# Attention, then a squared-ReLU layer pair: row maxima taken ten slots ahead, weighted sums in two parts, the seam between the stages overlapped

## The chip, the cores and the metric

One core of one Trainium2 chip runs the whole program. The metric is the device time of one execution in microseconds (us), lower is better. The engines are PE (TensorE, matrix products), DVE (VectorE), ACT (ScalarE), POOL (GpSimd) and SP (SyncE, which here only issues DMAs). Each of them runs its own instructions in program order and waits on semaphores of the others.

## What is computed

```python
def _attn_ref(q, k, v, g_q, g_k):          # q, k, v: 8 x 12 heads x 448 x 64, float32
    def rmsnorm(x, g):
        rms = np.sqrt(np.mean(x * x, axis=-1, keepdims=True) + 1e-06)
        return x / rms * g
    q_n, k_n = (rmsnorm(q, g_q), rmsnorm(k, g_k))
    scores = 1.0 / np.sqrt(64) * np.matmul(q_n, k_n.transpose(0, 1, 3, 2))
    scores = scores - np.max(scores, axis=-1, keepdims=True)
    attn = np.exp(scores)
    attn = attn / (np.sum(attn, axis=-1, keepdims=True) + 1e-09)
    return np.matmul(attn, v)

def _moe_ref(x, w_in, w_out, s, b):        # x: 3584 x 768, w_in: 768 x 2048, w_out: 2048 x 768
    r = np.maximum(x @ w_in, 0.0)
    return (s * (r * r) + b) @ w_out
```

The output of attention, 3584 tokens by 768, is the first operand of layer one.

## The kernel before

**Three stages.** Attention runs over 48 pairs of heads. Layer one (`ffn_in`, 8 batches of 448 tokens by 16 blocks of 128 columns, 128 blocks in all) follows it, then layer two (`multiply`, seven products of a blocked scheme for each 256 tokens). Weights and first operands of both layers are split in a high and a low float32r part, so each block of layer one is 18 matmuls.

**Slots.** Attention is written as a loop over slots, four to a pair (`W = 4`), from `FIRST = -14`. Slot i holds the work of one quarter of a pair, and `jobs` says which other steps are issued in it; all engines' orders are fixed by this program order (`manual_schedule`). In slot i:
- `score_t(i)` (L252, L256) makes a quarter of the transposed scores `st` on PE: a product of the scaled `kq`, then a second one that adds minus the row maxima, which lie as one row in a buffer `shq`. `exponent(i)` (L263) takes `exp` of it on ACT into `e`.
- `score(i + AHEAD)` (L223) makes a quarter of the untransposed scores `sh`, only for the maxima, and `maximum` (L232) reduces it on DVE into `nmx`. `sh` has one buffer in PSUM. `AHEAD` is 6.
- `shift` (L241) moves the four quarters of maxima of a pair into `shq` with two small DMAs, two slots before `score_t` first reads them. There are two `shq`, used in turn.
- in every fourth slot, `weigh` (L272, L279) makes the weighted sums of a pair and the sums of its exponentials (`av`): 16 products with v and 8 with ones, 24 in one run. `take` (L288, L289) copies them out on ACT.
- before and after a pair come its other steps: `load`, `norm` (L177, L182, L184, L185: squares on ACT, sums on DVE, the power -1/2 on POOL), `keep`, `load_kq`, `spread` (L201), `scale` (L205, L207, L211), `load_v`, then `gather` (L297, four small DMAs of the sums), `invert`, `put_z`, `get_z` (L314), `divide` (L320, POOL), `put_x` (L323).
- `convert` splits one of 24 pieces of w_in (a DMA `w64i` of 512 KB, L330) in every seventh slot, from slot 4 to slot 165.

**SP.** All DMAs are issued by SP in program order. A DMA waits there for the engine that makes its data, and each also for an earlier DMA on one of eight lanes, so the one eight places before it must have landed.

**The seam.** After the last slot the attention pools are closed. Then `x_load(0)` (L409) reads batch 0 of the attention's output and `x_split` (L416 on ACT, L417 on DVE) splits its six parts; the first block of layer one follows (L426). During layer one, `convert_out` splits w_out, 32 pieces spread over the first 103 blocks. In the last batch `t_step` prepares the sums of w_out for layer two: DMA, POOL (L514 to L516), ACT (L524), DVE (L532) in a chain.

## Time and profile before

| what | value |
|---|---|
| median of three runs | 1638.98 us (1638.83 to 1641.5) |
| the profiled execution | 1635.42 us, of which the span is 1633.4 us |
| busy share of the span | PE 90%, DVE 46%, ACT 41%, POOL 38% |
| attention, first transposed score to last weighted sum | 30.85 to 715.4 us |
| layer one, layer two begin at | 738.74 us, 1218.05 us |

The span runs from the first to the last instruction. A time line row says when a run of equal instructions on an engine began, how long it took, and in brackets how long the engine was idle before it and what ended that. PEclk is the granted clock of TensorE as a share of 2.4 GHz; its two levels are 1.0 (2.4 GHz) and 0.5 (1.2 GHz), and a mean lies between them. "DMA share" is the mean busy share of the core's 16 DMA engines.

### The profile page before, as it was taken

What the parts mean: (1) busy time and instruction counts of PE and PEld (TensorE: products, weight loads), DVE (VectorE), ACT (ScalarE), POOL (GpSimd) and SP (SyncE); (2) the same over time, 40 slices, a digit from 0 to 9 for tenths busy, and PEclk for the clock granted to TensorE, in tenths of its full rate; (3) what the DMA queues carried; (4) which work ended last, traced back from release to release, by engine and by line L of the source; (5) the groups of instructions that cost most, each with busy time, mean ns of one, the idle gap of its engine ahead of it and who ended that gap; (6) DMA issues with size and microseconds to landing.
All of it is one profiled execution on the core that took longest, in us unless ns stands there. A gap on an engine that the chain in (4) does not pass through costs nothing.

```text
span 1633.4 us, 23219 instructions
## 1 busy us (share of the span) xinstructions
PE 1474.5 (90%) x8536; PEld 1112.8 (68%) x8536; DVE 751.3 (46%) x1112; ACT 674.6 (41%) x1010; POOL 623.5 (38%) x536
## 2 busy tenths in 40 slices
PE   4888888888888888849999999999989999999999
PEld 3433333333333343418999999999979999999999
DVE  4444444454554444302222122221469677776775
ACT  3554555554555554322222222222355444444443
POOL 5554555555545654110000000000466555465553
PEclk6988889898988988879999999999999999999999
DMA  7566565656656565214434434442443333243331
GB/s 205 161 172 171 150 177 164 182 170 172 184 153 174 152 182 146 55 60 141 152 111 149 139 120 140 156 133 97 142 147 109 98 104 97 84 117 97 104 97 65
DMA packets 191234, 221.75 MB, mean 136 GB/s; under 512 B 69520, under 2 KB 162192, under 8 KB 191120
## 3 DMA queue, kind: packets, MB, share of 16 engines
q1 hardware_dynamic: 191120, 220.26, 45.9%
q8 instruction: 67, 1.10, 0.3%
q14 instruction: 47, 0.39, 0.1%
HBM read 161.48 MB, written 58.19 MB: 134 GB/s over the span
## 4 chain that ended last, share of the span: by engine, by line
PE 75%; DMA 11%; DVE 4%; SPq 4%; issue 2%; ACT 2%; POOL 2%; POOLq 0%; ACTq 0%; DVEq 0%
PE ph L426 26%; PE m L606 25%; PE av L272 9%; DMA shq<-nmx 6%; PE st L252 5%; PE st L256 4%; PE av L279 4%; DVE nmx L232 3%; PE sh L223 3%; SPq L297 3%; DMA raw<-in_dram 1%; DMA rb<-i_d 1%; DMA w<-w_d 1%; DMA i_d<-ri 1%; DVE t L532 1%
## 5 line engine op out<-in xcount | busy, mean ns | idle before, releaser
L426 PE MATMUL ph<-x,wih 128*128 128x448 f32 x1536 | 439.4, 367 | 23.3 <-DMA w64o<-in_dram 23.3
L606 PE MATMUL m<-t,gh 128*128 128x384 f32 x1568 | 400.9, 336 | 6.9 <-ACT gh L587 6.9
L232 DVE TENSOR_REDUCE nmx<-sh 112x2 fp32r<-112x896 f32 x192 | 207.8, 1082 | 357.9 <-PE sh L223 348.4
L426 PEld LDWEIGHTS ph<-x,wih 128*128 128x128 f32 x1536 | 289.2, 188 | 49.7 <-ACT x L416 24.1
L606 PEld LDWEIGHTS m<-t,gh 128*128 128x128 f32 x1568 | 284.8, 189 | 7.3 <-ACT gh L587 7.3
L426 PE MATMUL ph<-x,wil 128*128 128x448 f32 x768 | 281.9, 367 | 0.0
L256 PE MATMUL st<-shq,row 64*128 64x448 f32 x384 | 187.8, 782 | 91.0 <-DMA shq<-nmx 91.0
L606 PE MATMUL m<-t,gl 128*128 128x384 f32 x784 | 263.4, 336 | 0.1
L263 ACT ACTIVATE e<-st 128x896 f32<-128x896 f32 x192 | 176.0, 917 | 137.5 <-PE st L256 137.0
L252 PE MATMUL st<-kq 64*128 64x448 f32 x768 | 221.4, 624 | 0.2 <-ACT e L263 0.2
L444 ACT ACTIVATE r<-ph 128x448 f32<-128x448 f32 x128 | 69.6, 544 | 306.4 <-PE ph L426 193.2
L514 POOL TENSOR_TENSOR w<-w 128x384 f32<-128x384 f32 x13 | 17.0, 1305 | 442.0 <-DMA w<-w_d 436.6
L587 ACT CAST gh<-g 128x896 fp32r<-128x896 f32 x112 | 105.4, 942 | 178.3 <-POOL g L577 107.5
L256 PEld LDWEIGHTS st<-shq,row 64*128 64x128 f32 x384 | 65.3, 222 | 160.1 <-DMA shq<-nmx 137.6
L272 PE MATMUL av<-e,v 128*32 128x448 f32 x1536 | 172.3, 594 | 0.0
L588 DVE TENSOR_TENSOR gl<-g,gh 128x896 fp32r<-128x896 f32 x112 | 141.5, 1265 | 56.3 <-ACT gh L587 51.9
L573 POOL TENSOR_TENSOR g<-g 128x256 f32<-128x256 f32 x112 | 94.5, 844 | 179.2 <-DVE g L572 179.2
L417 DVE TENSOR_TENSOR x<-xr,x 128x448 fp32r<-128x448 f32 x48 | 29.6, 625 | 278.4 <-ACT x L416 261.2
L223 PE MATMUL sh<-kr 64*112 64x448 f32 x384 | 128.4, 532 | 32.2 <-DVE nmx L232 18.5
L426 PEld LDWEIGHTS ph<-x,wil 128*128 128x128 f32 x768 | 144.6, 188 | 12.7
L185 POOL TENSOR_TENSOR ri<-ri,mhalf 128x14 f32<-128x14 f32 x48 | 148.3, 3090 | 4.0
L606 PEld LDWEIGHTS m<-t,gl 128*128 128x128 f32 x784 | 147.8, 189 | 0.6 <-DVE gl L588 0.6
(63 smaller groups left out, 1465.8 us busy)
## 6 DMA issues: line engine op xcount, KB each, us to landing
r_d<-r SPq DMA_DIRECT2D x128, 224.0 KB, 2.0
raw<-in_dram SPq DMA_DIRECT2D x48, 448.0 KB, 5.9
kq<-in_dram SPq DMA_DIRECT2D x48, 448.0 KB, 4.8
rb<-i_d SPq DMA_DIRECT2D x96, 224.0 KB, 5.2
raw<-r_d SPq DMA_DIRECT2D x64, 256.0 KB, 2.8
v<-in_dram SPq DMA_DIRECT2D x48, 256.0 KB, 3.8
w64i<-in_dram SPq DMA_DIRECT2D x24, 512.0 KB, 5.8
w64o<-in_dram SPq DMA_DIRECT2D x32, 384.0 KB, 3.4
```

The lines of the kernel that those rows point to most:

```text
L185: G.tensor_tensor(ri, ri, mhalf[:, :n], ALU.pow)
L223: T.matmul(sh[:QC, j, :SEQ], t[d, 1].rearrange("k (p c) -> k c p", c=NQ)[:, c], t[d, 0], start=True, stop=True,)
L232: V.tensor_reduce(out=nmxs[p][:, :, c : c + 1], in_=shs.pop(i)[:QC, :, :SEQ], op=ALU.max, axis=AX.X, negate=True,)
L252: T.matmul(st[:, j, :SEQ], t[d, 0, k0 : k0 + P], t[d, 1], start=True, stop=False)
L256: T.matmul(st[:, j, :SEQ], row[d], shq[p % 2][d], start=False, stop=True)
L263: S.activation(e, sts.pop(i)[:, :, :SEQ], AF.Exp)
L272: T.matmul(t[n * Q : (n + 1) * Q, 0, :SEQ], x[:, kc, j, h * Q : (h + 1) * Q], e[kc][:, j], start=kc == 0, stop=kc == NKC - 1,)
L426: T.matmul(ph[:, :SEQ], w[:, cc, f0 : f0 + P], xs[b, cc][:, part, :], start=n == 0, stop=n == 3 * NCC - 1,)
L573: G.tensor_tensor(g9[:, 2:4], g9[:, 0:2], g9[:, 7:8].broadcast_to([P, 2, P]), ALU.add)
L587: S.copy(gh, g9[:, 1:8])
L588: V.tensor_tensor(gl, g9[:, 1:8], gh.bitcast(F32), ALU.subtract)
L606: T.matmul(to, g[:, sa], w, start=m == 0 and n == 0, stop=m == NM - 1 and n == 2,)
```

## The change

**In attention.** `AHEAD` becomes 10, and all steps before a pair move by four slots with it (`FIRST = -19`). `shift` stays at `s0 - AHEAD + W`, so it is now issued six slots before its first use; three `shq` instead of two, six `kq` instead of five. In even slots `score` stands ahead of `score_t`, in odd slots behind it, so the products for the maxima come in twos around the weighted sums. `weigh` is cut in two: part 0 (quarters 0 and 1) in slot 4p+3, part 1 (quarters 2 and 3) with `take` in slot 4p+5. `e` has one buffer for each quarter instead of two. The first four `sh` lie in four different places of PSUM. One multiplication of the first pair goes from POOL to DVE.

**At the seam.** `x_load(0)` is issued in slot 184 of 192 and the six `x_split` in slots 187 to 192, between the attention's own work. The slots after 193 (their DMAs, `invert`, `divide`) are issued between the first 16 blocks of layer one. `convert_out` starts four blocks later.

**At the end of layer one.** The last two blocks are run together, part by part of the first operand, and the splits for layer two stand ahead of their copies out of PSUM.

```diff
-FIRST = -14
-AHEAD = 6
+FIRST = -19
+AHEAD = 10
 STAGES = {
-    "raw": (-24, 0),
-    "norm": (-21, 1),
-    "keep": (-18, 3),
-    "kq": (-16, 1),
-    "spread": (-15, 4),
-    "scale": (-11, 5),
+    "raw": (-28, 0),
+    "norm": (-25, 1),
+    "keep": (-22, 3),
+    "kq": (-20, 1),
+    "spread": (-19, 4),
+    "scale": (-15, 5),
 }
...
-        shq = [ap.tile([P, SEQ], F32R, name=f"shq{n}") for n in range(2)]
+        shq = [ap.tile([P, SEQ], F32R, name=f"shq{n}") for n in range(3)]
...
+            tag = ("sh", "st0", "st1", "av")[i] if i < W else "sh"
+            sh = shs[i] = ps.tile([P, 2, 512], F32, tag=tag, name=f"sh{i}")
...
-            e = es[i] = ap.tile([P, 2, SEQ], F32, tag=f"e{kc}", bufs=2, name=f"e{i}")
+            e = es[i] = ap.tile([P, 2, SEQ], F32, tag=f"e{kc}", name=f"e{i}")
...
+            ahead = 0 <= i + AHEAD < NSLOT
+            if ahead and i % 2 == 0:
+                score(i + AHEAD)
             if 0 <= i < NSLOT:
                 score_t(i)
                 exponent(i)
-            if 0 <= i + AHEAD < NSLOT:
-                score(i + AHEAD)
+            if ahead:
+                if i % 2:
+                    score(i + AHEAD)
                 maximum(i + AHEAD)
...
-            if i % W == 1 and 0 <= (i - 5) // W < NPAIR:
-                weigh((i - 5) // W)
-                take((i - 5) // W)
+            if i % 2 and 0 <= (i - 3) // W < NPAIR:
+                p, g = divmod(i - 3, W)
+                weigh(p, g // 2)
+                if g:
+                    take(p)
...
     with tc.manual_schedule(engines=ORDERED):
-        x_load(0)
-        for cc in range(NCC):
-            x_split(0, cc)
+        for i in range(FIRST, NSLOT + 2):
+            slot(i)
+            if i == NSLOT - 8:
+                first.close()
...
+                x_load(0)
+            if NSLOT - 5 <= i < NSLOT + 1:
+                x_split(0, i - NSLOT + 5)
+        early.close()
...
         for n in range((B - 1) * NFC):
             b, fc = divmod(n, NFC)
             rectify()
             ffn_in(b, fc)
             keep_r()
+            if n < 16:
+                slot(NSLOT + 2 + n)
...
         rectify()
+        ffn_in(B - 1, NFC - 2, NFC - 1)
         keep_r()
```

On PE in the middle of attention, the rows of one pair (16) stood like this before; `st` is the transposed score, `sh` the score for the maxima, the number behind a name is the slot (for `av`, `kq`, `v` the pair):

```order
L223 MATMUL sh71_2200<-kr17_2044 112x448 x2
L272 MATMUL av15_2214<-e60_2055,v15_1954 32x448 x4
L272 MATMUL av15_2214<-e61_2082,v15_1954 32x448 x4
L272 MATMUL av15_2214<-e62_2132,v15_1954 32x448 x4
L272 MATMUL av15_2214<-e63_2153,v15_1954 32x448 x4
L279 MATMUL av15_2214<-e60_2055,ones_203 32x448 x2
L279 MATMUL av15_2214<-e61_2082,ones_203 32x448 x2
L279 MATMUL av15_2214<-e62_2132,ones_203 32x448 x2
L279 MATMUL av15_2214<-e63_2153,ones_203 32x448 x2
L252 MATMUL st66_2243<-kq16_1721 128x448 x2
L256 MATMUL st66_2243<-shq0_209,row_207 128x448 x2
L223 MATMUL sh72_2250<-kr18_2162 112x448 x2
```

And now:

```order
L228 MATMUL sh75_2259<-kr18_2090 112x448 x2
L278 MATMUL av15_2214<-e62_2181,v15_2013 32x448 x4
L278 MATMUL av15_2214<-e63_2199,v15_2013 32x448 x4
L285 MATMUL av15_2214<-e62_2181,ones_209 32x448 x2
L285 MATMUL av15_2214<-e63_2199,ones_209 32x448 x2
L228 MATMUL sh76_2289<-kr19_2208 112x448 x2
L257 MATMUL st66_2292<-kq16_1664 128x448 x2
L261 MATMUL st66_2292<-shq1_216,row_213 128x448 x2
L257 MATMUL st67_2311<-kq16_1664 128x448 x2
L261 MATMUL st67_2311<-shq1_216,row_213 128x448 x2
L228 MATMUL sh77_2318<-kr19_2208 112x448 x2
```

Between two `sh` there now lies either half of the weighted sums or two `st`; before there was one `st` between most of them and the whole of the weighted sums between two.

On SP in the same place, from the output of pair 24 (`x_d`) to the loads; before:

```order
L323 DMA x_d4_87<-u24_3488 128x448
L297 DMA zt26_3542<-sz26_3525 64x1x7 x4
L241 DMA shq0_209<-nmx28_3421 1x112x4 x2
L188 DMA i_d32_179<-ri32_3465 128x2x7
L314 DMA zb25_3563<-z_d25_116 64x448 x2
L215 DMA v29_3588<-in_2_dram 128x512
L195 DMA kq32_3590<-in_0_dram 128x896
L171 DMA raw34_3592<-in_1_dram 128x896
```

And now:

```order
L331 DMA x_d4_87<-u24_3547 128x448
L305 DMA zt26_3588<-sz26_3571 64x1x7 x4
L246 DMA shq2_217<-nmx29_3467 1x112x4 x2
L191 DMA i_d33_180<-ri33_3524 128x2x7
L322 DMA zb25_3609<-z_d25_116 64x448 x2
L219 DMA v29_3647<-in_2_dram 128x512
L198 DMA kq33_3649<-in_0_dram 128x896
L174 DMA raw35_3651<-in_1_dram 128x896
```

The order of the steps is the same; what stands behind the four `zt` of pair 26 is now the maxima of pair 29 instead of 28, and the loads of `kq` and `raw` are one pair further ahead.

On ACT at the seam, where `x0` is the split first operand of layer one and `ph` its product; before:

```order
L263 ACTIVATE e191_5757<-st191_5752 128x896
L288 COPY sz47_5793<-av47_5767 128x448
L289 COPY uz47_5792<-av47_5767 128x448
L416 CAST x0_0_5833<-xr0_5831 128x448
L416 CAST x0_1_5836<-xr0_5831 128x448
L416 CAST x0_2_5839<-xr0_5831 128x448
L416 CAST x0_3_5842<-xr0_5831 128x448
L416 CAST x0_4_5845<-xr0_5831 128x448
L416 CAST x0_5_5848<-xr0_5831 128x448
L444 ACTIVATE r0_0_5872<-ph0_0_5851 128x448
```

And now:

```order
L268 ACTIVATE e189_5738<-st189_5733 128x896
L296 COPY sz46_5756<-av46_5705 128x448
L297 COPY uz46_5755<-av46_5705 128x448
L419 CAST x0_2_5759<-xr0_5654 128x448
L268 ACTIVATE e190_5767<-st190_5762 128x896
L419 CAST x0_3_5775<-xr0_5654 128x448
L268 ACTIVATE e191_5783<-st191_5778 128x896
L419 CAST x0_4_5801<-xr0_5654 128x448
L419 CAST x0_5_5806<-xr0_5654 128x448
L296 COPY sz47_5825<-av47_5788 128x448
L297 COPY uz47_5824<-av47_5788 128x448
L447 ACTIVATE r0_0_5864<-ph0_0_5839 128x448
```

The six splits stand between the last exponentials, ahead of the copies of the last pair's sums.

## Rows read from the trace of the kernel before

**Rows 1.** Stretch 100 to 650 us: busy us (instructions) PE, PEld, DVE, ACT, POOL; clock, DMA share, GB/s.
```profile
100.00:650.00 550.00, 464.28 (x3063) 206.79 (x3063) 258.33 (x358) 285.62 (x387) 291.12 (x214) 0.88 0.61 170
```

**Rows 2.** The page: granted TensorE clock in 40 slices of 40.8 us.
```profile
PEclk6988889898988988879999999999999999999999
```

**Rows 3.** Who waited for whom, whole span: us in total, times, longest.
```profile
PE st L256 <- DMA shq<-nmx: 91.0, 75, 3.2
PE sh L223 <- DVE nmx L232: 18.5, 56, 1.8
PE m L606 <- ACT gh L587: 6.9, 1, 6.9
```

**Rows 4.** Time line of PE, one pair of attention: start, us, engine, line, tile.
```profile
486.72 0.57 PE L223 MATMUL sh<-kr 64*112 64x448 f32 x2 [0.24 <-DVE nmx L232]
487.21 3.21 PE L272 MATMUL av<-e,v 128*32 128x448 f32 x32
...
491.86 1.02 PE L252 MATMUL st<-kq 64*128 64x448 f32 x4
...
492.93 0.36 PE L223 MATMUL sh<-kr 64*112 64x448 f32 x2
493.13 0.91 PE L252 MATMUL st<-kq 64*128 64x448 f32 x4
...
498.59 0.47 PE L256 MATMUL st<-shq,row 64*128 64x448 f32 x1 [2.79 <-DMA shq<-nmx]
```

**Rows 5.** Time line of SP, same place: issues of DMAs.
```profile
493.70 0.33 SPq L323 DMA_DIRECT2D x_d<-u  x1
...
501.33 0.43 SPq L171 DMA_DIRECT2D raw<-in_dram  x1
...
503.00 1.40 SPq L201 DMA_DIRECT2D rb<-i_d  x2
```

**Rows 6.** DMA issues of the whole span: KB each, median us from issue to landing.
```profile
raw<-in_dram SPq DMA_DIRECT2D x48, 448.0 KB, 5.9
```

**Rows 7.** Time line of DVE, POOL and ACT, same place.
```profile
487.18 1.08 DVE L182 TENSOR_REDUCE ssq<-raw 128x14 f32<-128x896 f32 x1
...
488.64 3.93 POOL L185 TENSOR_TENSOR ri<-ri,mhalf 128x14 f32<-128x14 f32 x1
...
496.74 0.94 ACT L177 ACTIVATE raw<-raw 128x896 f32<-128x896 f32 x1
...
502.62 2.59 POOL L185 TENSOR_TENSOR ri<-ri,mhalf 128x14 f32<-128x14 f32 x1
505.17 1.14 POOL L320 TENSOR_TENSOR u<-uz,zb 128x448 f32<-128x448 f32 x1
```

**Rows 8.** Three stretches of two neighbouring pairs, columns as in Rows 1.
```profile
486.00:493.00 7.00, 6.76 (x62) 2.51 (x60) 4.09 (x7) 2.78 (x5) 4.57 (x3) 1.00 0.94 260
495.40:500.40 5.00, 2.04 (x10) 1.20 (x8) 1.03 (x2) 2.44 (x4) 1.68 (x2) 0.91 0.22 12
500.50:509.50 9.00, 9.00 (x70) 3.60 (x66) 4.20 (x7) 4.27 (x7) 6.09 (x5) 0.86 0.96 283
```

**Rows 9.** Time line at the start of attention.
```profile
30.32 0.73 PE L223 MATMUL sh<-kr 64*112 64x448 f32 x2 [1.19 <-DVE nmx L232]
...
30.85 1.70 PE L252 MATMUL st<-kq 64*128 64x448 f32 x4
...
32.44 0.94 ACT L211 CAST kr<-kq 128x896 fp32r<-128x896 f32 x1 [5.80 <-POOL kq L207]
```

**Rows 10.** Time line of PE at the seam between attention and layer one.
```profile
713.72 1.69 PE L279 MATMUL av<-e,ones 128*32 128x448 f32 x16
...
738.74 0.74 PE L426 MATMUL ph<-x,wih 128*128 128x448 f32 x1 [23.33 <-DMA w64o<-in_dram]
```

**Rows 11.** Time line of POOL and ACT before layer two.
```profile
1215.10 1.00 POOL L516 TENSOR_TENSOR w<-w 128x384 f32<-128x384 f32 x1
...
1217.06 1.78 ACT L587 CAST gh<-g 128x896 fp32r<-128x896 f32 x2
```

More of the change, by code (lines that the diff above doesn't have):

```diff
@@ L145, in constants, with attention @@
             nc.sync.dma_start(t, x.rearrange("(o d) -> o d", o=1).broadcast_to([P, 1]))
[L147 removed]
+    begun = []
+    def attention(ps):
+        ep = first.enter_context(tc.tile_pool(name="epool", bufs=1, side="right"))
         ones = ap.tile([P, 2, Q], F32, name="ones")
@@ L255, in score_t @@
                     else:
-                        T.matmul(st[:, j, :SEQ], row[d], shq[p % 2][d], start=False, stop=True)
+                        T.matmul(st[:, j, :SEQ], row[d], shq[p % 3][d], start=False, stop=True)
             if kc == W - 1:
@@ L359, in attention, with slot @@
             at(4 + 7 * n, convert, n)
-        begun = []
-        for i in range(FIRST, NSLOT + 16):
+        def slot(i):
             if i == FIRST:
@@ L380, in attention @@
                     begun.append(g)
-            if i % W == 1 and 0 <= (i - 5) // W < NPAIR:
-                weigh((i - 5) // W)
-                take((i - 5) // W)
-        assert not begun
-    with (
-        tc.tile_pool(name="apool", bufs=1) as ap,
-        tc.tile_pool(name="aps", bufs=1, space=PSUM) as aps,
-        tc.manual_schedule(engines=ORDERED),
-    ):
-        attention(ap, aps)
-    ps = ctx.enter_context(tc.tile_pool(name="ps", bufs=1, space=PSUM))
+            if i % 2 and 0 <= (i - 3) // W < NPAIR:
+                p, g = divmod(i - 3, W)
+                weigh(p, g // 2)
+                if g:
+                    take(p)
+        return slot
     free = [f"bank{i}" for i in range(8)]
@@ L671, in attention_then_relu2_ffn @@
             keep_r()
+            if n < 16:
+                slot(NSLOT + 2 + n)
+            else:
+                begun[:] = [g for g in begun if next(g, 0) is None]
             if fc == 1:
@@ L675, in attention_then_relu2_ffn @@
                 x_split(b + 1, fc // 2 - 2)
-            begun = [g for g in begun if next(g, 0) is None]
-            while started < len(todo_out) and started * 103 // len(todo_out) <= n:
+            while started < len(todo_out) and started * 103 // len(todo_out) + 4 <= n:
                 g = convert_out(started)
@@ L696, in attention_then_relu2_ffn @@
             g_load(x)
-        for n in range(NFC):
+        for n in range(NFC - 2):
             rectify()
```

126 lines of the change are left out of this document (69 added, 57 removed).

## The prediction

> **What bounds the kernel now.** I read the table of stretches first: in attention PE is busy 464 of 550 us at a mean clock of 0.88, and no other engine is busy for much over half of the time [rows 1]. In layers one and two the clock stands at 0.9 or more nearly throughout, while in attention it is mostly below 0.9 [rows 2]; so attention is the part with something to lose. The list of waits then says what PE stands still for: 91.0 us for the DMA that brings the maxima (`shq`), 18.5 us because the single `sh` buffer is still being reduced, and one stop of 6.9 us before layer two [rows 3]. The reader should see in the time line that a stop does more than its length: after the wait of 2.79 us at 498.59 [rows 4] the clock of the stretch is 0.91 and then 0.86 instead of 1.00 [rows 8]. At the seam PE is idle for 23.33 us [rows 10].
>
> **The period of a pair.** Attention goes from the first `st` at 30.85 [rows 9] to the last `av` at 713.72 + 1.69 = 715.4 [rows 10], 684.6 us for 48 pairs, 14.26 us each. What PE needs without a wait, at full clock, comes from starts in its time line [rows 4]: `sh` to `st` 492.93 to 493.13, 0.20; `st` to what follows 491.86 to 492.93, 1.07; `sh` to `av` 486.72 to 487.21, 0.49; the whole `av` 487.21 to 491.86, 4.65, so a half about 2.40 with its second change-over. Half a pair is now sh, st, st, sh, av: 0.20 + 2 x 1.07 + 0.49 + 2.40 = 5.23, a pair **10.46 us**. Of the 3.8 us above that today, 91.0 / 48 = 1.9 are the wait for `shq`, 18.5 / 48 = 0.4 that for `sh`, and the remaining 1.5 are work at half clock.
>
> **Part by part.**
> Ten slots ahead, three `shq`: the DMA is issued six slots before use instead of two. It still stands on SP behind `put_x` and the four `gather` DMAs, but six slots are over 15 us, so the wait for `shq` goes: -1.9 us a pair, and with it most of the half clock, -1.5.
> `sh` in twos: between two `sh` there are now 2 x 1.07 or 2.40 us of other PE work, more than a reduction's 1.1 us, so the wait for its buffer goes too: -0.4.
> `weigh` in two: the same 24 products; one more change-over, about 0.15 us, is in the 2.40. One `e` buffer: `exponent` then waits for the half of `weigh` that last read that quarter, but this half stands on PE ahead of the `st` that `exponent` needs anyway, so nothing is added; behind it on ACT only the copies and squares would wait. The sixth `kq` and the third `shq` cost one more memset on an idle POOL.
> What is late next is a chain through five engines. SP issues `put_x`, then `gather`, the maxima, `keep`, `get_z`, `v`, `kq`, `raw`; `raw` lands; ACT squares it, DVE sums it, POOL takes the power, then `divide`; and `put_x` of a pair two periods later waits for that. Its length: `put_x` to the issue of `raw` 493.70 to 501.33 [rows 5], 7.6 us with the issue of a weight piece in it, so 7.1 without; landing 5.9 [rows 6]; square 0.94, sum 1.08, 0.38 up to the power, the power 2.59 or 3.93, taken as 3.26, `divide` 1.14 [rows 7]; three hand-overs, 0.3 (estimate). That is 20.1 us for two periods, 10.1 each: just under the floor of PE. With a piece of w_in it is 0.5 more on SP and 2.0 more on the DMA engines (they are nearly full for 9.0 us in such a pair against 7.0 in one without [rows 8]): 22.6, or **11.3** each. Up to slot 164, where the loads for pairs end, there are 41 pairs and 24 pieces: 24 x 11.3 + 17 x 10.46 over 41 is 10.95. Because PE, this chain and SP (9.4 us of issues a pair: 493.70 to 501.76 is 8.1 with the piece, `put_z` about 0.4 and `spread` 1.4 follow [rows 5]) lie within a tenth of each other, each slip of one is passed on; I add 0.15 for that (estimate), **11.1 us**.
> On SP the row is plain: 8.1 us of issues without a break for transfers that the DMA engines carry in 7 to 9. The Trainium skill (DMA: Bandwidth & Descriptors, section Issuing engines are not separate DMA queues) says that the time a sequencer takes to start a DMA is usually small beside the DMA itself. By that rule SP would hold nothing up, and the time would be that of the floor below; the row speaks against it for this kernel.
> The power on POOL is the other open price: 3.93 every time makes the period 0.3 us longer, 2.59 every time as much shorter, 14 us in all either way. The Trainium skill (GPSIMD Engine Reference, section Key points) says that GpSimd shares its SBUF interfaces with VectorE and suffers from instructions there with two SBUF inputs. By that rule the denser DVE would bring the long power more often, and the time would lie at the 14 us more; the trace shows both lengths and does not decide how often.
> The start: `st` of slot 0 now stands behind eleven `sh`, the last three of pair 2, whose `kr` is ready at 32.44 + 0.94 [rows 9]. At 0.73 + 1.19 = 1.92 us for each `sh` [rows 9], slot 0 begins at about 33.4 + 2 x 1.92 + 0.2 = 37.4, 6.6 later than before.
> The last seven pairs have no loads beside them and the last ten slots no `sh`: 4.5 pairs at 10.46 and 2.5 at 2 x (2 x 1.07 + 2.40) = 9.1 make 69.8 us. The six splits for layer one lie there, on ACT and DVE that have lost the maxima and the loads; I cost them at nothing, and if they don't fit it is about 3 us, their own length in one run.
> The seam: the 23.33 us go. The first block may wait up to 1 us for a bank of PSUM that `take` empties, and gains about as much by the full clock; nothing in sum.
> Layer two: the 6.9 us stop ended with `gh` at 1217.06, which ACT runs behind casts that need POOL's sum of 1215.10 + 1.00 [rows 11]. The last two blocks in one free the buffer of `gh` earlier, but not that sum, so `gh` comes 0.3 us earlier at most. I take nothing; the bound is the whole stop, -7.
> `convert_out` four blocks later ends before layer one does, since its last piece begins at block 103 of 112 that it has: nothing.
>
> **The sum.** Layer one begins at 37.4 + 41 x 11.1 + 69.8 = 562.3 instead of 738.74. From there to the end it is 1633.4 - 738.7 = 894.7 as before: a span of 1457.0. Around the span lie 2.0 us (1635.42 against 1633.4), and the median of the runs is 3.6 above the profiled execution: 1457.0 + 5.6 = **1462 us**. All but the period is 1007.5 us; each 0.1 us of period is 4.1 us.
>
> **Rivals.**
> *PE alone sets the pace*: the chain gets by on its slack and every pair takes 10.46: 1007.5 + 41 x 10.46 = 1436. For it: without a weight piece the chain is 10.1. Against: 24 of 41 pairs have one. The page on DMAs named above would have this one.
> *Large and small transfers do not overlap*: today the DMA engines are full for 7.0 or 9.0 us and then, while SP issues the small DMAs, only 0.22 busy for 5.0 us, so 3.9 idle [rows 8]. If that order stays, a pair takes 8.2 + 3.9 = 12.1: 1504. For it: SP's order is the same. Against: the idle stretch is partly SP's waiting for POOL and ACT, which shrinks.
> *Another wait of the same size takes the place*, so that the maxima come early and the period stays 14.26: 1592, only seam and tail gained. Nothing in the waits but `shq` is that long.
> *Slower*: in the chain above `raw` must land before ACT squares it, three slots after its issue. If the denser transfers queue on the DMA engines, each us of landing costs half a us of period, 20.5 us in all. The kernel is slower from a period of (1642.3 - 1007.5) / 41 = 15.5 on, that is if `raw` lands 9.4 us later, at over 15 instead of 5.9; at 18 it would be about 1698. Against: the DMA engines are 0.61 busy [rows 1], and at 11.1 us would be 0.78.
>
> **Chances.** The forecast (period 10.8 to 11.5, 1450 to 1479) 0.57; PE alone 0.18; no overlap of transfers 0.16; same period 0.05; slower 0.04. The range goes from just under PE alone to just past the no-overlap case, 1434 to 1508, which also takes in the 14 us of the power and 20 us for a us of landing. A difference of 0.2% is about what a measurement of this kernel can tell from none. Faster by more 0.95, within 0.01, slower 0.04.
>
> **What would show it.** In the trace after: the wait of `st` for `shq` near zero and the clock of attention at 0.97 or more; `sh` hardly waiting; the first block of layer one within 2 us of the last `av`, at about 562; pairs with a weight piece longer than those without; and `put_x` on SP waiting for `divide`. Layer two's stop of about 7 us should still be there. It would be wrong if PE waits for `shq` still, if ACT waits for `raw` by several us in each pair, or if the clock stays below 0.95.

## The result, and the profile after

The changed kernel takes 1517.38 us (median of four runs, 1514.16 to 1525.77) against 1640.24 us of the kernel before on the same chip: a ratio of 0.9258, 95% interval 0.9217 to 0.9299. It is faster by 7.4%. The forecast was 1462, its range ended at 1508, so the direction held and the gain fell 55 us short. The execution profiled below is the slowest of the four (1525.77 us, span 1524.0 us).

Two lines of the page after, TensorE's granted clock and the DMA share in 40 slices of 38.1 us; they answer to [rows 2]:

```profile
PEclk6899999999999999999999999999989999999999
DMA  6666677776677663434434434334433333333331
```

From the third slice on, attention (it ends in the seventeenth) now runs at 0.9 or more. The table of stretches for 100 to 550 us (columns as in [rows 1]):

```profile
100.00:550.00 450.00, 378.24 (x2832) 173.05 (x2836) 246.71 (x331) 261.15 (x361) 272.95 (x198) 0.95 0.71 194
```

The clock is 0.95 instead of 0.88 and the DMA engines are busy 0.71 instead of 0.61 [rows 1], but PE is busy 378 of 450 us, still 84%. Where a half pair of PE runs undisturbed, it takes 5.00 us (time line of PE, from one `sh` to the same place half a pair later):

```profile
311.68 0.57 PE L228 MATMUL sh<-kr 64*112 64x448 f32 x2
...
316.68 0.58 PE L228 MATMUL sh<-kr 64*112 64x448 f32 x2
```

So PE's own floor is 10.0 us a pair, even below the forecast's 10.46. The waits of 100 to 550 us (total us, times, longest) say what is in its way:

```profile
ACT wih L104 <- DMA w64i<-in_dram: 71.4, 20, 6.8
DVE wai L102 <- DMA w64i<-in_dram: 69.8, 20, 5.8
PE sh L228 <- DVE nmx L237: 65.5, 35, 3.7
...
ACT kr L215 <- POOL kq L211: 55.5, 30, 4.1
...
POOL u L328 <- DMA zb<-z_d: 45.6, 23, 5.2
```

The wait of `st` for `shq`, 91.0 us before [rows 3], is gone from the list. In its place stand waits for a weight piece on two engines, for `kq`, for `zb`, and PE's wait for `sh` has grown from 18.5 over the whole span to 65.5 in these 450 us. The same view for SP's queue:

```profile
SPq L331 <- POOL u L328: 44.5, 29, 3.2
SPq L305 <- DMA raw<-in_dram: 22.2, 23, 2.0
SPq L305 <- DMA w64i<-in_dram: 8.4, 5, 2.2
```

The first is `put_x` waiting for `divide`. The other two are DMAs of `gather` (L305), whose data have nothing to do with `raw` or a piece of w_in: the fourth `gather` is the eighth DMA behind the last of these loads (where a piece stands in the row, the third is the eighth behind `raw`), and waits until it has landed.

The places in time. First `st`, last `av` and first block of layer one, first product of layer two, from the time line of PE:

```profile
42.32 0.73 PE L228 MATMUL sh<-kr 64*112 64x448 f32 x2 [1.19 <-DVE nmx L237]
42.85 1.69 PE L257 MATMUL st<-kq 64*128 64x448 f32 x4
...
551.36 0.91 PE L257 MATMUL st<-kq 64*128 64x448 f32 x4
...
622.71 0.94 PE L285 MATMUL av<-e,ones 128*32 128x448 f32 x8
624.73 0.47 PE L429 MATMUL ph<-x,wih 128*128 128x448 f32 x1 [1.09 <-ACT uz L297]
...
1108.16 1.01 PE L609 MATMUL m<-t,gh 128*128 128x384 f32 x2 [7.01 <-ACT gh L590]
```

The row at 551.36 is slot 164, counted back from the last slot. So the first 41 pairs took 551.36 - 42.85 = 508.5 us, **12.4 us each**, and the rest up to layer one 73.4. The seam is 1.09 us instead of 23.33 [rows 10], and layer two still stops 7.01 us.

### The profile page after: what moved, and what is told of

Same layout as the page of the kernel before. It is cut to its first block, busy times and chain, and to the rows that moved or that the text cites. A ratio compares the mean times of both kernels' runs of the same rounds, so it can differ in the third digit from the quotient of the medians.

```text
span 1524.0 us, 23381 instructions
## 1 busy us (share of the span) xinstructions
PE 1405.2 (92%) x8536; PEld 1082.5 (71%) x8536; DVE 760.2 (50%) x1113; ACT 666.8 (44%) x1010; POOL 625.3 (41%) x536
## 4 chain that ended last, share of the span: by engine, by line
PE 74%; DMA 15%; POOL 3%; DVE 3%; SPq 3%; issue 2%; ACT 1%; DVEq 0%; POOLq 0%; ACTq 0%
PE ph L429 28%; PE m L609 27%; PE av L278 7%; PE st L257 5%; DMA raw<-in_dram 4%; DMA w64i<-in_dram 4%; PE av L285 3%; PE sh L228 3%; DMA zt<-sz 2%; PE st L261 1%; DVE nmx L237 1%; DMA v<-in_dram 1%; DMA zb<-z_d 1%; DMA w<-w_d 1%; POOL u L328 1%
## 5 line engine op out<-in xcount | busy, mean ns | idle before, releaser
L268 ACT ACTIVATE e<-st 128x896 f32<-128x896 f32 x192 | 171.9, 913 | 59.0 <-PE st L261 57.7
L228 PEld LDWEIGHTS sh<-kr 64*112 64x112 f32 x384 | 55.5, 277 | 198.6 <-issue 60.6
L228 PE MATMUL sh<-kr 64*112 64x448 f32 x384 | 96.0, 492 | 105.1 <-DVE nmx L237 80.4
L257 PE MATMUL st<-kq 64*128 64x448 f32 x768 | 185.1, 555 | 0.0
L261 PE MATMUL st<-shq,row 64*128 64x448 f32 x384 | 143.6, 733 | 0.0
L188 POOL TENSOR_TENSOR ri<-ri,mhalf 128x14 f32<-128x14 f32 x48 | 136.4, 2841 | 4.0
```

The lines of the kernel that those rows point to most:

```text
L188: G.tensor_tensor(ri, ri, mhalf[:, :n], ALU.pow)
L228: T.matmul(sh[:QC, j, :SEQ], t[d, 1].rearrange("k (p c) -> k c p", c=NQ)[:, c], t[d, 0], start=True, stop=True,)
L257: T.matmul(st[:, j, :SEQ], t[d, 0, k0 : k0 + P], t[d, 1], start=True, stop=False)
L261: T.matmul(st[:, j, :SEQ], row[d], shq[p % 3][d], start=False, stop=True)
L268: S.activation(e, sts.pop(i)[:, :, :SEQ], AF.Exp)
```

## The experiments

Ratios are against the kernel before, with their 95% intervals; "attention" is the first `st` to the first `ph` in the profiled execution, given where the text uses it.

| run | median us | ratio | attention us |
|---|---|---|---|
| changed kernel | 1517.38 | 0.9258 [0.9217, 0.9299] | 581.9 |
| e1 piece six slots ahead | 1512.55 | 0.9238 [0.9205, 0.9271] | 577.0 |
| e2 one piece only | 1488.37 | 0.9078 [0.9046, 0.9110] | 548.0 |
| e3 seam undone | 1547.47 | 0.9436 [0.9392, 0.9480] | 608.6 |
| e4 six slots ahead | 1526.54 | 0.9318 [0.9283, 0.9352] | 597.4 |
| e5 store of u later | 1533.28 | 0.9350 [0.9315, 0.9386] | 596.3 |
| e6 three DMAs less | 1698.51 | 1.0356 [1.0318, 1.0394] | |
| e7 e5 and e6 | 1684.90 | 1.0281 [1.0232, 1.0330] | |
| e8 weigh whole | 1525.53 | 0.9296 [0.9255, 0.9338] | 595.5 |
| e10 cast after square | 1517.52 | 0.9272 [0.9234, 0.9311] | |
| e11 e10 and e1 | 1512.06 | 0.9219 [0.9190, 0.9249] | |
| e12 gather on ACT | 1544.77 | 0.9431 [0.9390, 0.9471] | |
| e13 gather in two | 1499.46 | 0.9143 [0.9110, 0.9175] | 563.7 |
| e14 e13 and e10 | 1503.65 | 0.9172 [0.9148, 0.9195] | |
| e15 e13, e10 and e5 | 1509.66 | 0.9208 [0.9190, 0.9226] | |
| e16 one DMA more | 1545.16 | 0.9418 [0.9378, 0.9457] | 605.8 |
| e17 e13, e10, e5 and e1 | 1507.99 | 0.9189 [0.9164, 0.9215] | 579.2 |
| **e18 e13 and e1** | **1497.00** | **0.9124 [0.9104, 0.9145]** | **559.3** |
| e19 e13, e5 and e1 | 1509.30 | 0.9207 [0.9178, 0.9237] | |

**First four: what each part is worth.** After the profile, theory 1 was that the waits for weight pieces are the missing 55 us, theory 2 that SP's order and the transfers are.

```diff
             nc.sync.dma_start(w.rearrange("p n t -> p (n t)"), src)
-            for _ in range(3):
+            for _ in range(6):
                 yield
```

> The changed kernel, but each piece of w_in is first used six slots after its load was issued instead of three; the same DMAs in the same order. Theory 1 (ACT and DVE, in order, stand at the first use of a piece that has not landed, 71 and 70 us in all, and the maxima and PE wait behind them): these waits fall below 10 us, the period of a pair from 12.5 to about 10.8, the time to 1445 to 1465. Theory 2 (SP's order lets large and small transfers not overlap, which sets a period of 12.1): the waits go, others take their place, 1500 to 1520.

Measured 1512.55, an interval that overlaps that of the changed kernel. Every wait of ACT and DVE for a piece is gone from the list, and this one (same view, 100 to 550 us) has taken the place:

```profile
ACT kr L215 <- POOL kq L211: 99.3, 35, 5.7
```

Theory 1 falls: 141 us of waits on two engines were worth 5 us in the medians, which the intervals do not tell from nothing.

```diff
+        one = {}
...
-            w = ep.tile([P, WI, 2], I32, tag="w64", bufs=2, name=f"w64i{n}")
-            nc.sync.dma_start(w.rearrange("p n t -> p (n t)"), src)
+            if n == 0:
+                w = one["w"] = ep.tile([P, WI, 2], I32, tag="w64", name=f"w64i{n}")
+                nc.sync.dma_start(w.rearrange("p n t -> p (n t)"), src)
+            w = one["w"]
```

> The changed kernel, but only the first piece of w_in is loaded and all 24 conversions work on it (the output leaves out the other pieces); ACT and DVE do the same work. It has neither the waits nor the 11.5 MB of transfers. Theory 1: as the kernel with the later use or up to 15 us less, 1435 to 1460. Theory 2: the large transfers of a pair shrink by 2.0 us in 23 pairs, so 46 us less than the changed kernel, 1465 to 1475, and clearly less than the kernel with the later use.

Measured 1488.37, outside both forecasts: without 23 of the 24 transfers 29 us go. More than their waits (e1), but not the 55, so a period above PE's floor is there without them too. The edit takes out the issues of these 23 DMAs with their bytes, so it does not tell the two apart.

```diff
-        for i in range(FIRST, NSLOT + 2):
+        for i in range(FIRST, NSLOT + 18):
...
-                x_load(0)
-            if NSLOT - 5 <= i < NSLOT + 1:
-                x_split(0, i - NSLOT + 5)
+        x_load(0)
+        for cc in range(NCC):
+            x_split(0, cc)
...
-            if n < 16:
-                slot(NSLOT + 2 + n)
-            else:
+            if True:
```

> The changed kernel with the seam as before: all slots are run out, then batch 0 is loaded and split, then layer one begins. It prices the seam: if the gap comes back as it was, PE is idle for about 23 us there again and the time is 20 to 25 us more than the changed kernel, 1537 to 1543; by either theory of the period the same.

Measured 1547.47, 30 us more, a little above what was written down. PE's stop at the seam is back:

```profile
651.61 0.74 PE L429 MATMUL ph<-x,wih 128*128 128x448 f32 x1 [22.33 <-ACT x L419]
```

So the seam gives what was forecast (23.3); the 7 us beyond that lie within the two intervals.

```diff
-FIRST = -19
+FIRST = -14
-AHEAD = 10
+AHEAD = 6
...
-    "raw": (-28, 0),
+    "raw": (-24, 0),
```

(the other five stages move by four slots too)

> The changed kernel with the maxima six slots ahead again (all steps before a pair moved back with them); weighted sums in two parts, the order of the products and the seam stay changed. It prices the ten slots. If the early maxima carried the gain, the wait for the maxima is back with some 1.9 us a pair and the half clock with it, 1570 to 1610; if another wait sets the period anyway (theory 2), it stays within 1510 to 1530.

Measured 1526.54, 9 us more, with intervals that just overlap: the second outcome written down. The wait is back, in the list of 100 to 550 us,

```profile
PE st L261 <- DMA shq<-nmx: 52.5, 36, 3.7
```

and yet attention is only 15.5 us longer, of which 10.3 are given back at the start (first `st` at 32.57 instead of 42.85). So the wait that the change was made for stood, by then, for little more than what stood behind it.

**Opening loops one at a time.** Theory A: the loop through `put_x`. Theory B: SP's issues and the transfers.

```diff
-            at(s0 + 14, put_x, p)
+            at(s0 + 16, put_x, p)
...
-            u = us[p] = lp.tile([P, SEQ], F32, tag="u", bufs=2, name=f"u{p}")
+            u = us[p] = lp.tile([P, SEQ], F32, tag="u", bufs=3, name=f"u{p}")
```

> The store of u (put_x) stands two slots later in SP's row, with a third buffer for u; nothing else is changed. In the changed kernel SP waits 44.5 us at that store for POOL's divide in 100 to 550 us, 29 times, and everything behind it in the row (gather, the maxima, the loads of the next pair) waits with it. Theory A (the period is the loop SP's store, loads, raw, power, divide, store): the store then asks for a u that was due two slots before, the loop has half a pair of slack, SP's wait there goes nearly to zero and the period falls from 12.1 to 11.0 to 11.4: 1472 to 1490 us. Theory B (the period is SP's own issues and the stretch in which only small transfers run, whatever SP waits for): the wait turns up at another place of SP or as a longer stretch of idle DMA engines, 1508 to 1522 us.

Measured 1533.28: slower, and outside both forecasts. SP's waits in 100 to 550 us:

```profile
SPq L246 <- DMA raw<-in_dram: 34.9, 24, 2.3
SPq L305 <- DMA kq<-in_dram: 19.1, 29, 1.2
```

and the landing of `raw` there (count, KB, median us), to be held against 6.5 in the changed kernel:

```profile
raw<-in_dram SPq DMA_DIRECT2D x35, 448.0 KB, 7.2
```

The wait for `u` (44.5) is gone from the list, and these two waits for DMAs eight places back are 54 us, where the changed kernel had 27 for `raw` and `kq`. `put_x` now stands behind `gather`, so the eighth after `raw` is the first of the maxima (L246), and that is where the wait moved: the count of eight holds in a second order. The store of 224 KB, which was issued ahead of the small DMAs, is now issued with the loads, and `raw` lands in 7.2 instead of 6.5 us. Theory A falls; of B, the wait did turn up at another place of SP, but the time is 11 us above its range.

```diff
-            for j in range(2):
-                for h in range(2):
-                    n = (2 * h + j) * Q
+            for h in range(2):
+                n = 2 * h * Q
                     nc.sync.dma_start(
-                        zt[j * D : (j + 1) * D, h],
-                        sz[n : n + 1].rearrange("o (p c) -> o p c", c=TILES),
+                    zt[:, h], sz[n : n + Q + 1 : Q].rearrange("j (p c) -> j p c", c=TILES)
...
-            for j in range(2):
-                nc.sync.dma_start(
-                    zb[j * D : (j + 1) * D], z_d[p][j : j + 1].broadcast_to([D, SEQ])
+            r = z_d[p].rearrange("j (o s) -> j o s", o=1)
+            nc.sync.dma_start(zb, r.broadcast_to([2, D, SEQ]))
```

> The same bytes in three DMAs less for each pair: gather issues two of two rows each instead of four of one row, get_z one instead of two. In the changed kernel the four cost SP 2.4 us and the two 1.1 to 1.2 us, so 1.6 to 1.8 us of SP's row go for each pair. Theory A (loop through the power and divide, two periods long, with this stretch of SP in it once): 0.8 to 0.9 us less a pair, 1480 to 1487 us. Theory B (SP's issues are the stretch in which the large transfers stand still): the whole 1.6 to 1.8 us go from each pair until PE's floor of 10.0 to 10.5 is reached, 1445 to 1462 us. If neither SP nor the loop sets the period: 1510 to 1520.

Measured 1698.51, 181 us more than the changed kernel. Neither theory has that. One stretch of the table of stretches:

```profile
318.00:323.00 5.00, 3.37 (x14) 2.07 (x14) 4.77 (x6) 3.08 (x4) 0.29 (x1) 0.50 0.14 38
```

and one piece of the chain of waits (start, us, what):

```profile
340.23 11.00 DMA zb<-z_d
```

For five us the DMA engines are 0.14 busy at 38 GB/s, that is two or so of sixteen, and the chain stands 11.00 us on a `zb` whose two halves land in 3.6 us each in the changed kernel. The edit had put a dimension of size two outermost in a transfer of 224 KB. The Trainium skill (DMA: Bandwidth & Descriptors, section Why a DMA increments its semaphore by 16 and not by 1) says that a DMA is split over the largest number of engines, up to 16, that divides the slowest dimension (of a size above one) on both of its sides; by that rule two engines carry it, and the share of 0.14, 2.2 of sixteen, agrees. So this run was no test of the number of issues.

The two edits together:

```diff
-            at(s0 + 14, put_x, p)
+            at(s0 + 16, put_x, p)
...
+            nc.sync.dma_start(zb, r.broadcast_to([2, D, SEQ]))
```

> The two edits before together: the store of u two slots later and three DMAs less for each pair. Theory A: the loop is cut and the next limit is PE at 10.0 to 10.5 or the loads with weight pieces, 1445 to 1470 us, clearly below the run with the late store alone. Theory B: as the run with fewer issues alone, within 8 us. If the two gains add in full, PE's floor cuts them off at about 1440.

Measured 1684.90, spoiled by the same transfer (and 14 us below e6, so what the late store costs elsewhere cannot be read from this pair).

```diff
-            if i % 2 and 0 <= (i - 3) // W < NPAIR:
-                p, g = divmod(i - 3, W)
-                weigh(p, g // 2)
-                if g:
-                    take(p)
+            if i % W == 1 and 0 <= (i - 5) // W < NPAIR:
+                p = (i - 5) // W
+                weigh(p, 0)
+                weigh(p, 1)
+                take(p)
```

> The weighted sums of a pair stand again in one piece, in the slot where their second half stands in the changed kernel, with two buffers for the first two quarters of e; the ten slots ahead, the sh in twos and the seam stay. Theory: PE's own order does not set the period (PE is busy 378 of 450 us), so the time stays within 10 us of the changed kernel, 1507 to 1527. Rival: the halves are what takes out PE's remaining waits, because a whole sum of 4.65 us holds back the two st buffers and so exponent, whose quarter of a pair is then longer: 0.5 to 1 us a pair, 1535 to 1560 us.

Measured 1525.53; the intervals overlap. Whole sums cost 8 us or nothing, as was written down.

Theory C was a loop of one pair without any DMA: POOL's `kq`, `kr` on ACT, behind it the square, `ssq`, the power, `divide`, the next `kq`. It explained why `kr` waits for `kq` in e1.

```diff
             yield
             yield
+            yield
             kr = krs[p] = ep.tile([P, 2, SEQ], F32R, tag="kr", bufs=2, name=f"kr{p}")
```

> The cast kr on ACT stands one slot later, so that the square of raw stands ahead of it on ACT and no longer behind it; nothing else is moved. Theory C: the period of the changed kernel is a loop of one pair through three engines and no DMA at all: POOL's two kq, then kr on ACT, behind it in ACT's row the square, then ssq on DVE, the power, (the low half of a weight piece,) divide and the next kq on POOL. Its steps in the traces: kq 2.24 to 3.1, kr 0.94, square 0.9, up to the start of ri 1.3 to 1.4, ri 0.29, power 2.59 or 3.97, divide 1.14, together 9.5 to 11.7, and 1.28 more where a weight piece's low half lies between: 11 to 12.5, which is the period seen, with and without the pieces' loads. With the square ahead of the cast this loop is open. Theory C: ACT's waits of kr for kq may stay, but the period falls to 10.6 to 11.4, 1455 to 1488 us. Theory B (SP's issues and its full lanes with the transfers set the period): nothing gained, 1508 to 1522.

Measured 1517.52, as the changed kernel. ACT's waits of 100 to 550 us:

```profile
ACT raw L180 <- DMA raw<-in_dram: 72.7, 31, 6.0
```

The wait of `kr` for `kq` (55.5) left the list, and the one of the square for `raw` is 72.7 where the changed kernel has 11.7. Theory C falls.

```diff
-            for _ in range(3):
+            for _ in range(6):
...
+            yield
             kr = krs[p] = ep.tile([P, 2, SEQ], F32R, tag="kr", bufs=2, name=f"kr{p}")
```

> The square ahead of the cast, and each weight piece loaded six slots before its first use instead of three. Theory C: with the loop open, ACT's and DVE's waits for a weight piece (71.4 and 69.8 us in the changed kernel) are the next stops, and taking them out now pays where it paid only 5 us alone: 10 to 25 us below the run with the cast alone, 1440 to 1470. Theory B: within 6 us of the run with the piece alone, 1507 to 1519.

Measured 1512.06, as the earlier piece alone.

```diff
-                    nc.sync.dma_start(
+                    nc.scalar.dma_start(
                         zt[j * D : (j + 1) * D, h],
```

> The four small DMAs that gather the row sums of a pair are issued by ACT, right behind the copy that writes them, instead of by SP; the same bytes. SP loses 2.4 to 3.5 us of its row in each pair, with the waits for its eighth DMA back that stood there. ACT takes the issues on, at 58% busy. Theory B (SP's issues and lanes set the period): 1 to 1.7 us less a pair, 1448 to 1478 us. Theory C (a loop through POOL, ACT and DVE without SP): no gain, 1505 to 1525, and slower by up to 20 if each issue holds ACT up for as long as it does SP, since ACT's row is in the loop.

Measured 1544.77. The longest of ACT's waits in 100 to 550 us, and the landing of `raw` there:

```profile
ACT e L268 <- DMA zt<-sz: 69.1, 16, 6.8
```

```profile
raw<-in_dram SPq DMA_DIRECT2D x35, 448.0 KB, 5.1
```

`raw` lands sooner (5.1 for 6.5), but the gather's issues and their waits now hold ACT, up to 6.8 us, and the exponents with it. B falls. C had up to 20 us more if the issues hold ACT up; it was 27.

**The number of DMAs.** Theory D: the count of eight closes a loop on SP's row. `raw` must land before the eighth DMA behind it is issued, and from there the row runs on to the next `raw`.

```diff
-            for j in range(2):
-                for h in range(2):
-                    n = (2 * h + j) * Q
+            for h in range(2):
+                n = 2 * h * Q
                     nc.sync.dma_start(
-                        zt[j * D : (j + 1) * D, h],
-                        sz[n : n + 1].rearrange("o (p c) -> o p c", c=TILES),
+                    zt[:, h], sz[n : n + Q + 1 : Q].rearrange("j (p c) -> j p c", c=TILES)
```

> gather issues two DMAs of two rows each instead of four of one row; get_z stays at two. So 14 DMAs for a pair without a weight piece instead of 16. Theory D: SP issues no DMA before the one eight back has landed; in the changed kernel the eighth after raw is the last gather, and raw's landing of 6.5 us and SP's issues from there to the next raw (0.6 + 1.2 + 0.5 + 1.2 + 0.6 + 0.4 + 0.5 = 5.0) close a loop of 11.5 us, about 12.5 with a weight piece, whose load is then the one that is waited for. With 14 the eighth after raw is the second of the maxima, and the loop is 6.5 + 3.8 = 10.3, a us more with a piece: 0.6 to 1.2 us less a pair, 1465 to 1492 us. Rival: a gather DMA of two rows lands late, as get_z did when it was made one DMA, and the z values come late: 1515 to 1600. Rival: neither SP nor its waits set the period: 1508 to 1524.

Measured 1499.46: 18 us less, 0.44 a pair, in the direction of D and short of its size. SP's waits:

```profile
SPq L329 <- POOL u L326: 54.7, 33, 3.6
...
SPq L246 <- DMA raw<-in_dram: 4.7, 6, 1.8
```

The wait for `raw` fell from 22.2 to 4.7, and moved to the maxima as D has it; the wait for `u` grew by 10. SP's own issues also fell by two of about 0.6 us a pair, so D's count of eight is not separated here from the bare time of issuing.

```diff
+            yield
             kr = krs[p] = ep.tile([P, 2, SEQ], F32R, tag="kr", bufs=2, name=f"kr{p}")
```

> Gather in two DMAs and the cast kr behind the square on ACT. If theory D holds, SP's loop is about 10.3 to 11.3 and the loop through POOL's kq, kr, square, sum, power and divide (9.5 to 12) is the next limit, which the late cast opens: 8 to 25 us below the run with the gather alone, 1445 to 1480. If theory D does not hold: within 6 us of the run with the gather alone.

> Gather in two DMAs, the cast behind the square, and the store of u two slots later with a third buffer. Under theory D three loops of nearly the same length lie on each other (SP's eight in flight, the one through POOL and ACT, the one through the store of u), and only with all three open the floor of PE with the weight pieces' stops is left: 1440 to 1470 us, below each run that opens one. Without theory D: no lower than the run with two edits.

(e15 adds the two lines of e5.) Measured 1503.65 and 1509.66: opening the other loops on top gave nothing, against what D had written down for them (at most 1480 and 1470). With the late store it is 6 us more than without, in intervals that touch, and 10 us more than e13, in intervals that do not.

```diff
+    n_d = [dpool.tile([P, TILES], F32, name=f"n_d{p}") for p in range(NPAIR)]
...
+            nc.sync.dma_start(n_d[p], mhalf[:, :TILES])
```

> One DMA more for each pair behind the spread of the norms: 3.5 KB of a constant to a place in DRAM that nobody reads; SP's issue of it is about 0.4 us and nobody waits for it. Theory D: it moves the DMA that waits for raw from the fourth gather to the third, so that the loop takes in one issue of 0.6 and its own 0.4: 0.6 to 1.0 us more a pair, 1540 to 1560 us. Rival (SP's row has slack, since it stands 40.1 us at the store of u anyway): 1512 to 1525.

Measured 1545.16, 28 us or 0.7 a pair more, as D has it. SP's waits:

```profile
SPq L307 <- DMA raw<-in_dram: 31.3, 29, 1.9
SPq L333 <- POOL u L330: 18.9, 16, 2.4
```

A DMA of 3.5 KB that nobody reads costs about what its issue takes on SP (0.58 to 0.62 us in the time line of 300 to 340 us). The wait before `put_x` shrinks to 18.9, and the time grows all the same: that wait was no slack. The wait for `raw` grows from 22.2 to 31.3. This run too changes the issues and the count of eight together.

**All together.**

```diff
-            for _ in range(3):
+            for _ in range(6):
...
+            yield
             kr = krs[p] = ep.tile([P, 2, SEQ], F32R, tag="kr", bufs=2, name=f"kr{p}")
...
-            at(s0 + 14, put_x, p)
+            at(s0 + 16, put_x, p)
```

(on the kernel of e13; e18 has the first hunk alone, e19 the first and the third)

> All four edits: gather in two DMAs, cast behind the square, store of u two slots later, each weight piece loaded six slots ahead instead of three. If the pieces' landing (DVE 67 us, ACT 53 us, and behind DVE SP's 36 us for the maxima, in 100 to 500 of the run without it) is the last closed loop, the period falls to 10.5 to 11.2 and the time to 1455 to 1488. If the transfers themselves are the limit (the pieces' and the pairs' bytes at the rate the DMA engines reach while they are full), the wait moves to ACT's raw or POOL's zb and the time stays at 1500 to 1512.

> Gather in two DMAs and pieces six slots ahead; the cast and the store of u as in the changed kernel. If the pieces' landing is the last loop by itself: 1470 to 1490. If the loops through the cast and the store of u close at the same length: 1492 to 1500, the 5 us that the earlier pieces gained alone.

> Gather in two DMAs, store of u two slots later, pieces six slots ahead; the cast as in the changed kernel. If the loop through the cast (11 to 12.5 with a piece's low half in it) is as long as the others: 1495 to 1505, and only the run with all four edits falls below. If it is not: as the run with all four, within 6 us.

Measured 1507.99, 1497.00 and 1509.30. With all four opened the wait is ACT's, for `raw`, 11.7 us in the changed kernel:

```profile
ACT raw L180 <- DMA raw<-in_dram: 150.2, 35, 7.6
```

For e17 it is the second outcome written down, which put it down to the transfers; but the DMA share of e17 is 0.70 in 100 to 550 us, against 0.75 in e18, so that the DMA engines themselves are the limit is not shown. The late store costs 12 us here (e19 against e18). **e18 is the fastest** of the kernels that compute everything, 1.3% below the changed kernel, with intervals that do not meet (0.9104 to 0.9145 against 0.9217 to 0.9299); from e13 (0.9110 to 0.9175) it is not told apart.

## Why the prediction was right and where it was wrong

**Right.** The wait for `shq` went, the seam fell to 1.09 us, layer two's stop stayed, `put_x` waits for `divide`, and the period is set outside PE, with SP's row in it.

**Signs that failed.** `sh` was to hardly wait: PE waits 65.5 us for it. The forecast took 0.4 us a pair off, from the spacing on PE and a reduction of 1.1 us; it left out that DVE works in order and stands at the weight pieces (69.8 us) ahead of the maxima. The clock of attention is 0.95, not 0.97. Pairs with a weight piece were to be longer: from one issue of `raw` to the next, 36 rounds from 88 to 544 us, it is 12.7 us on average with a piece in it and 12.6 without.

**The sum against the trace.** Layer one begins at 624.73 instead of 562.3, 62.4 us late. The start is 5.5 of it (42.85 against 37.4: the eleven `sh` stand on PE as forecast, but DVE reduces them behind other sums, so some wait 2.66 to 3.90 us instead of 1.19). The last seven pairs are 3.6 (73.4 against 69.8). The other **53.3 us are the period of the first 41 pairs, 12.4 instead of 11.1**. From layer one on it is 899.3 instead of 894.7, 4.6 more, in an execution that is 8.4 above the median where the sum added 3.6. 62.4 + 4.6 - 12.0 is the miss of 55. The 4.6 belong to this one execution: in the profiles of the experiments the same stretch takes 888 to 892 us. So the whole miss lies in attention.

**The step that failed** is the period of 11.1: the forecast took one chain through five engines as the longest, put 0.15 us (an estimate) for the waits of that chain, SP and PE on each other, and closed no loop with the limit on DMAs in flight. With it failed the weight given to the rival "large and small transfers do not overlap", which had a period of 12.1 and 1504 us. Four neighbouring stretches of the changed kernel, two pairs (columns as in [rows 8], the last but one is the DMA share):

```profile
301.00:304.40 3.40, 0.57 (x8) 0.00 (x0) 2.29 (x5) 2.46 (x5) 0.64 (x2) 1.00 0.21 20
304.40:311.50 7.10, 6.46 (x40) 3.32 (x40) 4.47 (x6) 2.25 (x3) 7.10 (x4) 0.76 0.95 271
311.50:315.00 3.50, 3.50 (x28) 1.91 (x28) 2.10 (x2) 2.89 (x4) 0.58 (x1) 1.00 0.25 50
315.00:325.20 10.20, 9.17 (x74) 4.06 (x66) 4.75 (x8) 5.71 (x9) 7.33 (x6) 1.00 0.90 259
```

The pattern of [rows 8] is still there: 3.4 us with hardly a transfer, 7.1 full, 3.5 nearly idle, 10.2 full with a weight piece. By these bounds that is 10.5 and 13.7 us, 12.1 on average. The forecast said against it that the idle stretch is partly SP's waiting, which shrinks. It shrank from 5.0 to 3.5 and no further, and SP's row shows why (time line of SP, the same place):

```profile
309.06 0.33 SPq L331 DMA_DIRECT2D x_d<-u  x1
309.48 2.42 SPq L305 DMA_DIRECT2D zt<-sz  x4
312.00 1.22 SPq L246 DMA_DIRECT2D shq<-nmx  x2
313.27 0.58 SPq L191 DMA_DIRECT2D i_d<-ri  x1
313.90 1.11 SPq L322 DMA_DIRECT2D zb<-z_d  x2
315.11 0.53 SPq L219 DMA_DIRECT2D v<-in_dram  x1
315.74 0.38 SPq L198 DMA_DIRECT2D kq<-in_dram  x1
316.17 0.42 SPq L174 DMA_DIRECT2D raw<-in_dram  x1
```

From the end of `put_x` (309.39) to the issue of `v` (315.11) SP issues nothing large for 5.7 us, without any wait in it: seven tiny DMAs and the two of `zb`. And it cannot run far ahead, since the fourth gather must wait for the `raw` eight places back to land, which took (issues of 100 to 550 us: count, KB, median us)

```profile
raw<-in_dram SPq DMA_DIRECT2D x36, 448.0 KB, 6.5
```

The count of eight was stated in the text on the kernel before; the forecast closed no loop with it. Closed, it is the landing of `raw`, 6.5 us, plus the issues from 311.3 to 316.17, 4.9: 11.4 us without a wait elsewhere. That is 0.3 more than the forecast's 11.1; the measured 12.4 is a further 1.0 above it.

The forecast's own chain was nearly right in size. 309.06 to 316.17 is indeed 7.1; the landing is 6.5 instead of 5.9, the power 2.89 on average instead of 3.26, `divide` 1.49 instead of 1.14. That makes 20.7 us for two periods where it had 20.1, or 0.3 a pair. What it had no term for are the waits on the way. `divide` was to follow the power; in 23 of 36 pairs it waits for `zb` instead, 45.6 us in all (0.8 us in the same stretch before):

```profile
L328 POOL TENSOR_TENSOR u<-uz,zb 128x448 f32<-128x448 f32 x36 | 53.8, 1493 | 45.6 <-DMA zb<-z_d 45.6
```

And SP's row, 9.4 us of issues a pair in the forecast, carries 44.5 us of waits for `u` and 40 for earlier DMAs in these 36 pairs, 1.2 and 1.1 a pair. How much of the last 1.0 us each of them makes was not measured.

**What the runs show of it.** The number of SP's DMAs counts (two less 18 us less, one more 28 us more), and so do the pieces' transfers or their issues (e2, 29 us less). Waits on ACT and DVE hardly do: taken out they gave 0 to 5 us (e1, e10, e11), and another wait of the same alternation took the place. Putting a large store among the loads costs 6 to 16 us (e15 against e14, e19 against e18, e5). The period that attention still has in e2, (548.0 - 73.4) / 41 = 11.6 us if its end is as long as here, is near the 11.4 of this loop.

**The two rules weighed in the forecast.** The Trainium skill (DMA: Bandwidth & Descriptors, section Issuing engines are not separate DMA queues) has the time a sequencer takes to start a DMA as usually small beside the DMA. The forecast made of it the time of PE alone, 1436. One issue is small beside its DMA here too (0.58 us of a landing of 6.2 for the tiny DMA of e16), but 16 in one row add up, and e13 and e16 show that they count. By the rule of the Trainium skill (GPSIMD Engine Reference, section Key points) that GpSimd suffers from VectorE's instructions with two inputs in SBUF, the long power was to come more often with a denser DVE. The mean of the power in the groups of POOL, 100 to 550 us, went the other way, to 2.89 us from 3.15 (100 to 650 us before):

```profile
L188 POOL TENSOR_TENSOR ri<-ri,mhalf 128x14 f32<-128x14 f32 x36 | 104.0, 2889 | 3.0
```

The traces bear the rule itself out, by what runs on DVE at the same time. In the time lines of 60 to 600 us before, all 17 long powers have one of the three steps of a weight piece with two inputs in SBUF beside them (L106, L108, L114), and none of the 21 short ones has; so that trace did show when the long one comes, which the forecast left open. In the changed kernel all 9 long ones have one, and so have 8 of the 31 short ones. `divide` took 1.13 to 1.15 us in all 37 pairs of that stretch before; now 14 of 42 take 1.37 to 2.54, each with such a step beside it, and the other 28 keep their length without one. One of the 14:

```profile
421.81 2.44 POOL L328 TENSOR_TENSOR u<-uz,zb 128x448 f32<-128x448 f32 x1
422.56 0.68 DVE L114 SCALAR_TENSOR_TENSOR wai<-wih,wai 128x512 f32<-128x512 f32 x1
```

So the power got shorter by 0.26 us on average and `divide` longer by 0.35: in the forecast's chain the two nearly cancel, and the miss is not their doing.

**Open.** Of the 126 us by which attention is shorter (707.9 to 581.9, the seam in it), the seam is 27 (e3), the ten slots 16 (e4) and the halves 14 (e8) when undone one at a time, in single profiled executions. The rest was not attributed: the order of `sh` in twos was not undone alone, and two parts may each stand in for the other. And with all four loops opened (e17) the alternation stays, at 579.2 us of attention; which coupling keeps it then was not settled. Nor did a run change the time of SP's issues without their number, or the count of eight alone. e18, the best, is still 35 us above the forecast. An order in which large and small DMAs alternate in SP's row was not tried.

## What to carry to other kernels

Before sizing what a removed wait gives, close every loop of the new steady state, also those through the limit on DMAs in flight: landing of a transfer, plus the issues from the DMA that waits for it to the same transfer of the next round. Where one queue issues a burst of large DMAs and then a row of tiny ones, look at the DMA share in the two stretches; if the DMA engines are nearly idle in the small row (0.25 for 3.5 us here), count the issues and leave a large store among the small ones. A wait of 70 us on an engine can be worth next to nothing if what it waits for is the slow end of such a loop. And where several loops have nearly the same length, do not take the longest and next to nothing for the rest: here 1.0 of the 1.3 us a pair that the forecast lacked lies above every loop that was closed.

## What the runs showed of the hardware

- One DMA of 224 KB with a dimension of two outermost (e6) held up everything behind it: a share of 0.14 of the DMA engines for 5 us, 11.00 us in the chain for one of them, and 181 us in the program (199 against e13, which has the other edit of e6 alone). In two DMAs, with 64 outermost, the same bytes land in 3.6 us.
- The gather of two rows, also with two outermost, did no harm (e13): it carries 3.5 KB.
- Tiny DMAs issued behind large ones land late (100 to 550 us of the changed kernel, in brackets the same stretch before): the store `z_d` of 3.5 KB, right behind `raw`, in 6.7 us (5.1), as long as `raw` with 448 KB, 6.5 (5.9); `zt` of 1.8 KB, behind the store of `u`, in 4.0 (1.9). The maxima of 1.8 KB, behind the `zt`, hardly changed: 2.0 (1.9).
- The power on POOL kept two lengths in all kernels, 2.6 to 2.9 and 3.7 to 4.1 us, with nothing between. In the kernel before and the changed one the long one came only beside a DVE instruction with two inputs in SBUF.
